# Attention and two projections merged into one hand-set TensorE order

## The chip, the core and the metric

The kernel runs on one core of one Trainium2 chip. The metric is the device time of one execution in microseconds (us); lower is better. The engines are named as the profile names them: PE is TensorE (PEld its weight loads), DVE is VectorE, ACT is ScalarE, POOL is GpSimd, SP is the engine that issues most of the DMAs.

## The reference

Inputs `q`, `k`, `v` are float32 of shape (8, 12, 448, 64): 8 batches, 12 heads, 448 positions, 64 channels. `w_in` is (768, 2048), `w_out` is (2048, 768).

```
q_n, k_n = rmsnorm(q, g_q), rmsnorm(k, g_k)       # x / sqrt(mean(x*x) + 1e-6) * g, over the 64 channels
scores   = q_n @ k_n.T / sqrt(64)                 # per batch and head: 448 x 448
attn     = softmax(scores);  o = attn @ v         # 448 x 64
x        = o of all heads side by side            # (3584 tokens, 768)
h        = x @ w_in                               # (3584, 2048)
g        = h * sigmoid(1.702 * h)
out      = g @ w_out                              # (3584, 768)
```

## The kernel before

The work falls into two stages, one after the other.

**Attention.** The unit is a pair of heads of one batch: 8 batches of 6 pairs make 48 pairs. The 448 positions are cut into 4 chunks of 112 rows. For each pair `phase1` issues four loads of q and k on SP (line 137), squares them on POOL (L143), sums the squares on DVE (L147) and loads v, cast to bf16, by two DMAs issued on POOL (L153). When all six pairs of a batch have their sums, `do_rsqrt` takes the reciprocal roots with integer and float steps on DVE (`_rsqrt_bits`, L26 to L38). `stage_T` scales q and k on POOL (L190), transposes them by 8 PE instructions (L199) and copies the result out of PSUM on DVE (L203). `stage_S` makes the scores in 4 chunks of keys: two matmuls with 64 contraction rows each, one for each head, in the two halves of the array (L214), then one exp on ACT for both heads (L221). `stage_Omm` multiplies the exps with v: 32 matmuls a pair, each with 112 columns of exps as weights and 65 moving columns (64 channels and a column of ones that gives the softmax sum, L231). `stage_Otail` divides on DVE (L244, L245), transposes back (4 PE instructions, L253) and copies into `xT` on ACT (L257). So a pair has 8 + 8 + 32 + 4 = 52 PE matmuls.

**Projections.** After all 48 pairs, in 7 blocks of 512 tokens: `gp` = 16 groups of 6 matmuls with `w_in_s` as weights and 512 moving columns (L311), sigmoid-gelu on ACT (L318), then `op` = 8 groups of 16 matmuls of 384 columns with the gelu output as weights (L328), a copy on ACT (L336), a store on SP (L337).

The order on each engine is set by a scheduler that takes the instructions by priority and by what they wait for; the program order of the loop over `gi` is the priority. Tiles come from pools with a number of buffers each; an instruction that writes a buffer waits until its last reader is done. PSUM has 8 banks; in the attention stage 4 of them are the two score buffers.

Of the kernel before, what the change touches and what calls it, by code (L numbers as in the profile page):

```python
# [13 lines left out]
AX = mybir.AxisListType  # L14

RSQRT_NEWTON = 2
_MAGIC = 0x5F3759DF


def _rsqrt_bits(nc, eng, out_ap, in_ap, magic_ap, tmp_pool, n_newton=2, tag=""):  # L20
    free_shape = list(in_ap.shape)
    sl = tuple(slice(0, d) for d in free_shape)
    x_int = in_ap.bitcast(I32)
    y = tmp_pool.tile(free_shape, FP32, tag="rsq_y" + tag, name="rsq_y")
    y_int = y[sl].bitcast(I32)
    eng.tensor_scalar(out=y_int, in0=x_int, scalar1=1, scalar2=None,  # L26
                      op0=ALU.arith_shift_right)
    eng.tensor_tensor(out=y_int, in0=magic_ap, in1=y_int, op=ALU.subtract)
    yf = y[sl]
    t = tmp_pool.tile(free_shape, FP32, tag="rsq_t" + tag, name="rsq_t")  # L30
    tf = t[sl]
    for i in range(n_newton):
        dst = out_ap if i == n_newton - 1 else yf
        eng.tensor_tensor(out=tf, in0=yf, in1=yf, op=ALU.mult)
        eng.tensor_tensor(out=tf, in0=tf, in1=in_ap, op=ALU.mult)
        eng.tensor_scalar(out=tf, in0=tf, scalar1=-0.5, scalar2=1.5,
                          op0=ALU.mult, op1=ALU.add)
        eng.tensor_tensor(out=dst, in0=yf, in1=tf, op=ALU.mult)  # L38
    if n_newton == 0:
        eng.tensor_copy(out=out_ap, in_=yf)  # L40
# [3 lines left out]
def kernel(  # L44
# [12 lines left out]

# [4 lines left out]
    NT = B * S  # L62
    SS = 112
    NS = S // SS
    NP = H // 2

    consts = ctx.enter_context(tc.tile_pool(name="consts", bufs=1))
    xt_pool = ctx.enter_context(tc.tile_pool(name="xt", bufs=1))
    wpool = ctx.enter_context(tc.tile_pool(name="w", bufs=1))

    ident = consts.tile([128, 128], BF16)
    make_identity(nc, ident)

    magicA = consts.tile([128, NP, 2, 2, NS], I32)
    nc.vector.memset(magicA[:, :, :, :, :], _MAGIC)

    gq128 = consts.tile([128, 1], FP32)
    gk128 = consts.tile([128, 1], FP32)
    gq_r = g_q.rearrange("(d o) -> d o", o=1)
    gk_r = g_k.rearrange("(d o) -> d o", o=1)  # L80
    nc.sync.dma_start(out=gq128[0:64, :], in_=gq_r)
    nc.sync.dma_start(out=gq128[64:128, :], in_=gq_r)
    nc.sync.dma_start(out=gk128[0:64, :], in_=gk_r)
    nc.sync.dma_start(out=gk128[64:128, :], in_=gk_r)
    gG = consts.tile([128, 1], FP32)
    nc.vector.tensor_tensor(out=gG[:, :], in0=gq128[:, :], in1=gk128[:, :],
                            op=ALU.mult)
    nc.vector.tensor_scalar(out=gG[:, :], in0=gG[:, :], scalar1=8.0,
                            scalar2=None, op0=ALU.mult)
    magicG = consts.tile([128, 1], I32)  # L90
    nc.vector.memset(magicG[:, :], _MAGIC)
    rs_pool = ctx.enter_context(tc.tile_pool(name="rs_const", bufs=1))
    gG_rs = consts.tile([128, 1], FP32)
    _rsqrt_bits(nc, nc.vector, gG_rs[:, :], gG[:, :], magicG[:, :], rs_pool,
                n_newton=3, tag="G")
    sqrtG128 = consts.tile([128, 1], FP32)
    nc.vector.reciprocal(out=sqrtG128[:, :], in_=gG_rs[:, :])

    w_in_s = wpool.tile([128, DM // 128, DF], BF16)
    nc.gpsimd.dma_start(  # L100
        out=w_in_s[:, :, :],
        in_=moe_w_in.rearrange("(ko p) f -> p ko f", p=128),
    )
    w_out_s = wpool.tile([128, DF // 128, DM], BF16)
    nc.gpsimd.dma_start(
        out=w_out_s[:, :, :],
        in_=moe_w_out.rearrange("(ko p) f -> p ko f", p=128),
    )

    xT = xt_pool.tile([128, DM // 128, NT], BF16)  # L110

    attn_pools = ExitStack()
    araw = attn_pools.enter_context(tc.tile_pool(name="a_raw", bufs=NP + 3))
    vraw = attn_pools.enter_context(tc.tile_pool(name="a_v", bufs=NP + 4))
    asqp = attn_pools.enter_context(tc.tile_pool(name="a_sq", bufs=2))
    astat = attn_pools.enter_context(tc.tile_pool(name="a_stat", bufs=2))
    asn = attn_pools.enter_context(tc.tile_pool(name="a_sn", bufs=3))
    asb2 = attn_pools.enter_context(tc.tile_pool(name="a_sb2", bufs=3))
    aobs = attn_pools.enter_context(tc.tile_pool(name="a_obs", bufs=2))

    ps_t = attn_pools.enter_context(
        tc.tile_pool(name="a_ps_t", bufs=1, space=bass.MemoryType.PSUM))
    ps_s = attn_pools.enter_context(
        tc.tile_pool(name="a_ps_s", bufs=2, space=bass.MemoryType.PSUM))
    ps_o = attn_pools.enter_context(
        tc.tile_pool(name="a_ps_o", bufs=2, space=bass.MemoryType.PSUM))
    ps_ot = attn_pools.enter_context(
        tc.tile_pool(name="a_ps_ot", bufs=1, space=bass.MemoryType.PSUM))

    def phase1(b, p, ssq):  # L130
        h0 = 2 * p
        qk_raw2 = araw.tile([128, 2, 2, NS, D], FP32, tag="qk_raw2",
                            name="qk_raw2")
        src = (q, k)
        for g in range(2):
            for hp in range(2):
                nc.sync.dma_start(  # L137
                    out=qk_raw2[:SS, g, hp, :, :],
                    in_=src[g][b, h0 + hp].rearrange(
                        "(ss ns) d -> ss ns d", ns=NS),  # L140
                )
        sqv = asqp.tile([128, 2, 2, NS, D], FP32, tag="sq", name="sq")
        nc.gpsimd.tensor_tensor(out=sqv[:SS, :, :, :, :],  # L143
                                in0=qk_raw2[:SS, :, :, :, :],
                                in1=qk_raw2[:SS, :, :, :, :],
                                op=ALU.mult)
        nc.vector.reduce_sum(out=ssq[:SS, p, :, :, :],  # L147
                             in_=sqv[:SS, :, :, :, :], axis=AX.X)
        v_ext2 = vraw.tile([128, 2, NS, D + 1], BF16, tag="v_ext2",
                           name="v_ext2")  # L150
        nc.gpsimd.memset(v_ext2[:SS, :, :, D:D + 1], 1.0)  # L151
        for hp in range(2):
            nc.gpsimd.dma_start(  # L153
                out=v_ext2[:SS, hp, :, :D],
                in_=v[b, h0 + hp].rearrange("(ss ns) d -> ss ns d", ns=NS),
            )
        return qk_raw2, v_ext2

    class BState:
        __slots__ = ("ssq", "aa", "qk", "vx")  # L160

        def __init__(self):
            self.ssq = astat.tile([128, NP, 2, 2, NS], FP32, tag="ssq",
                                  name="ssq")
            self.aa = None
            self.qk = [None] * NP
            self.vx = [None] * NP

    def do_rsqrt(st):
        st.aa = astat.tile([128, NP, 2, 2, NS], FP32, tag="aa", name="aa")  # L170
        _rsqrt_bits(nc, nc.vector, st.aa[:SS, :, :, :, :],
                    st.ssq[:SS, :, :, :, :], magicA[:SS, :, :, :, :], astat,
                    n_newton=RSQRT_NEWTON)

    states = [None] * (B + 1)
    states[0] = BState()
    for p in range(NP):
        qk, vx = phase1(0, p, states[0].ssq)
        states[0].qk[p] = qk
        states[0].vx[p] = vx  # L180
    do_rsqrt(states[0])

    def stage_T(b, i, st):
        qk_n2 = asn.tile([128, 2, NS, 2, D], BF16, tag="qkn", name="qkn")
        for g in range(2):
            in0 = st.qk[i][:SS, g, :, :, :].rearrange(
                "ss hp ns d -> ss ns hp d")
            in1 = st.aa[:SS, i, g, :, :].rearrange(
                "ss hp ns -> ss ns hp").to_broadcast([SS, NS, 2, D])
            nc.gpsimd.tensor_tensor(  # L190
                out=qk_n2[:SS, g, :, :, :],
                in0=in0,
                in1=in1,
                op=ALU.mult,
            )
        t_ps = ps_t.tile([128, 2, NS, SS], BF16, tag="tp", name="t_ps")
        for g in range(2):
            for s in range(NS):
                nc.tensor.transpose(t_ps[:128, g, s, :SS],  # L199
                                    qk_n2[:SS, g, s, :, :],  # L200
                                    ident[:SS, :SS])
        qkT = asb2.tile([128, 2, NS, SS], BF16, tag="qkT", name="qkT")
# [37 lines left out]
    def stage_Otail(b, i, oph):  # L240
# [11 lines left out]
        for qs in range(NS):  # L252
            nc.tensor.transpose(ot_ps[:128, qs, :SS], obs2[:SS, qs, :, :],  # L253
                                ident[:SS, :SS])
# [116 lines left out]
```

## Time and profile before

| | |
|---|---|
| median of 3 runs | 697.98 us (696.99 to 698.12) |
| span of the profiled execution, first to last instruction | 696.5 us |
| profiled execution's own time | its span and about 1.5 us around it, if it was like the median |
| PE busy | 618.6 us (89%), 4064 matmuls |
| DVE, ACT, POOL busy | 178.1, 313.5, 263.5 us |
| first matmul, first projection matmul, last matmul ends | 62.5, 398.9, 692.0 us |

A busy share is the time in which an engine had an instruction in work. For PE it says little of the speed: the instructions are pipelined, their ends are modelled, and a matmul at a slower array clock is busy for longer. So the prediction counts the distance between starts.

### The profile page before, as it was taken

Reading aid. Unit: us, or ns where it says so; the run is one execution under the profiler, and the core shown is the slowest. Engines: PE = TensorE matmul, PEld = TensorE weight load, DVE = VectorE, ACT = ScalarE, POOL = GpSimd, SP = SyncE. Lnnn points to the kernel's source line nnn. Section 1 sums busy time; section 2 is a strip of 40 time slices with the busy share of each in tenths; the row PEclk is TensorE's granted clock in tenths of the full one; section 3 lists DMA queues with packets and bytes.
Section 4 is the critical chain, followed back from the end, with each engine's and each line's share of the span. In section 5 each row is a group of like instructions: output and inputs, shape, how many; then the busy total and the mean of one; then the engine's idle time right before and its main releaser. Section 6 shows DMA issues by size and latency. Waiting matters only on the chain.

```text
span 696.5 us, 9788 instructions
## 1 busy us (share of the span) xinstructions
PE 618.6 (89%) x4064; PEld 386.2 (55%) x4064; DVE 178.1 (26%) x387; ACT 313.5 (45%) x382; POOL 263.5 (38%) x296
## 2 busy tenths in 40 slices
PE   0002799999999999999999999999999999999997
PEld 0001477677776767677777745555464554545554
DVE  1146463745347373633422200000000000000000
ACT  0001567666666666767676652332413233141331
POOL 1478959789595978959530000000000000000000
PEclk9999999999999999999999999999999999999999
DMA  8995627365362736434200001102011010101101
GB/s 152 234 244 79 123 20 147 45 122 73 53 137 18 143 50 116 78 31 84 14 1 1 1 1 47 46 0 91 1 46 45 24 69 0 69 24 46 46 23 70
DMA packets 76365, 45.48 MB, mean 65 GB/s; under 512 B 48416, under 2 KB 71968, under 8 KB 76320
## 3 DMA queue, kind: packets, MB, share of 16 engines
q0 software_dynamic: 47392, 11.80, 17.4%
q1 hardware_dynamic: 28928, 33.05, 15.3%
q8 instruction: 32, 0.52, 0.3%
q14 instruction: 13, 0.11, 0.0%
HBM read 45.61 MB, written 11.01 MB: 81 GB/s over the span
## 4 chain that ended last, share of the span: by engine, by line
PE 60%; POOL 19%; issue 8%; DMA 7%; DVE 5%; SPq 1%; ACT 0%; POOLq 0%; ACTq 0%
PE gp L311 21%; PE op L328 21%; PE o_ps L231 9%; POOL qkn L190 8%; POOL sq L143 7%; DMA qk_raw<-in_k_dram 6%; PE sc_ps L214 6%; POOL v_ext L153 4%; PE t_ps L199 2%; DVE rsq_y L26 2%; DVE ssq L147 1%; PE ot_ps L253 1%; DMA qk_raw<-in_q_dram 1%; POOL v_ext L151 0%; SPq L137 0%
## 5 line engine op out<-in xcount | busy, mean ns | idle before, releaser
L221 ACT ACTIVATE att<-sc_ps 112x896 bf16<-112x896 f32 x192 | 175.6, 921 | 175.6 <-PE sc_ps L214 174.2
L231 PEld LDWEIGHTS <-att 112*112 112x112 bf16 x1536 | 159.3, 210 | 36.3 <-issue 32.8
L231 PE MATMUL o_ps<-v_ext,att 112*112 112x65 bf16 x1536 | 175.7, 283 | 0.4 <-ACT att L221 0.3
L311 PE MATMUL gp<-xT,w_in_s 128*128 128x512 bf16 x672 | 148.3, 382 | 0.0
L328 PE MATMUL op<-w_out_s,g_tile 128*128 128x384 bf16 x896 | 146.7, 326 | 0.0
L328 PEld LDWEIGHTS <-g_tile 128*128 128x128 bf16 x896 | 87.7, 98 | 58.7
L214 PE MATMUL sc_ps<-qkT 64*112 64x448 bf16 x384 | 118.4, 617 | 0.8 <-DVE qkT L203 0.8
L199 PE MATMUL t_ps<-ident,qkn 112*128 112x112 bf16 x384 | 54.8, 295 | 68.6 <-POOL qkn L190 63.7
L311 PEld LDWEIGHTS <-w_in_s 128*128 128x128 bf16 x672 | 66.2, 99 | 79.2 <-issue 1.9
L190 POOL TENSOR_TENSOR qkn<-qk_raw,aa 112x512 bf16<-112x512 f32 x96 | 99.2, 1055 | 25.3 <-PE t_ps L199 13.3
L143 POOL TENSOR_TENSOR sq<-qk_raw 112x1024 f32<-112x1024 f32 x48 | 90.8, 1897 | 29.1 <-DMA qk_raw<-in_k_dram 27.4
L318 ACT ACTIVATE g_tile<-gp 128x512 bf16<-128x512 f32 x112 | 66.8, 597 | 74.7 <-PE gp L311 74.6
L199 PEld LDWEIGHTS <-qkn 112*128 112x128 bf16 x384 | 33.9, 136 | 97.5 <-POOL qkn L190 68.3
L336 ACT COPY osb<-op 128x768 f32<-128x768 f32 x28 | 22.4, 799 | 125.0 <-PE op L328 125.0
L147 DVE TENSOR_REDUCE ssq<-sq 112x16 f32<-112x1024 f32 x48 | 58.4, 1216 | 73.8 <-POOL sq L143 73.8
L153 POOL DMA_DIRECT2D v_ext<-in_v_dram x96 | 69.0, 723 | 11.0 <-POOL v_ext L151 10.1
L257 ACT COPY xT<-ot_ps 128x448 bf16<-128x448 bf16 x48 | 55.2, 1150 | 3.4 <-PE ot_ps L253 3.4
L203 DVE TENSOR_SCALAR qkT<-t_ps,sqrtG 128x896 bf16<-128x896 bf16 x48 | 32.6, 680 | 40.9 <-PE t_ps L199 40.9
L214 PEld LDWEIGHTS <-qkT 64*112 64x112 bf16 x384 | 31.8, 165 | 18.9 <-issue 8.3
L244 DVE RECIPROCAL rcp<-o_ps 112x4 f32<-112x4 f32 x96 | 17.0, 179 | 92.9 <-PE o_ps L231 92.9
L245 DVE TENSOR_TENSOR obs<-o_ps,rcp 112x256 bf16<-112x256 f32 x96 | 39.8, 420 | 1.5
L253 PE MATMUL ot_ps<-ident,obs 112*128 112x112 bf16 x192 | 27.6, 294 | 3.7 <-DVE obs L245 3.7
(28 smaller groups left out, 74.6 us busy)
## 6 DMA issues: line engine op xcount, KB each, us to landing
qk_raw<-in_q_dram SPq DMA_DIRECT2D x96, 112.0 KB, 2.3
qk_raw<-in_k_dram SPq DMA_DIRECT2D x96, 112.0 KB, 2.7
out_dram<-osb SPq DMA_DIRECT2D x28, 384.0 KB, 2.3
v_ext<-in_v_dram POOLq DMA_DIRECT2D x96, 56.0 KB, 2.9
w_in_s<-in_moe_w_in_dram POOLq DMA_DIRECT2D x1, 3072.0 KB, 21.3
w_out_s<-in_moe_w_out_dram POOLq DMA_DIRECT2D x1, 3072.0 KB, 40.8
gq<-in_g_q_dram SPq DMA_DIRECT2D x2, 0.2 KB, 2.3
gk<-in_g_k_dram SPq DMA_DIRECT2D x2, 0.2 KB, 8.0
```

The source lines that it names most:

```text
L143: nc.gpsimd.tensor_tensor(out=sqv[:SS, :, :, :, :], in0=qk_raw2[:SS, :, :, :, :], in1=qk_raw2[:SS, :, :, :, :], op=ALU.mult)
L147: nc.vector.reduce_sum(out=ssq[:SS, p, :, :, :], in_=sqv[:SS, :, :, :, :], axis=AX.X)
L153: nc.gpsimd.dma_start(out=v_ext2[:SS, hp, :, :D], in_=v[b, h0 + hp].rearrange("(ss ns) d -> ss ns d", ns=NS),)
L190: nc.gpsimd.tensor_tensor(out=qk_n2[:SS, g, :, :, :], in0=in0, in1=in1, op=ALU.mult,)
L199: nc.tensor.transpose(t_ps[:128, g, s, :SS], qk_n2[:SS, g, s, :, :], ident[:SS, :SS])
L214: nc.tensor.matmul(sc_ps[:SS, hp, :S], lhsT=qkT[lo:lo + 64, 1, kc, :SS], rhs=qkT[lo:lo + 64, 0, :, :], start=True, stop=True,)
L221: nc.scalar.activation(out=att2[:SS, kc, :, :], in_=sc_ps[:SS, :, :S], func=ACT.Exp)
L231: nc.tensor.matmul(oph[hp][:SS, qs, :D + 1], lhsT=att2[:SS, kc, hp, qs * SS:(qs + 1) * SS], rhs=st.vx[i][:SS, hp, kc, :D + 1], start=(kc = ...
L257: nc.scalar.copy(out=dst, in_=ot_ps[:, :, :])
L311: nc.tensor.matmul(gp[:, :], lhsT=w_in_s[:, ki, m * 128:(m + 1) * 128], rhs=xT[:, ki, tok0:tok0 + NTC], start=(ki == 0), stop=(ki == KI - 1),)
L318: nc.scalar.activation(out=g_tile[:, m, :], in_=gp[:, :], func=ACT.Gelu_apprx_sigmoid,)
L328: nc.tensor.matmul(op[:, half, :HALF], lhsT=g_tile[:, ko, tm * 128:(tm + 1) * 128], rhs=w_out_s[:, ko, half * HALF:(half + 1) * HALF], sta ...
```

## The change

It rewrites the kernel as one loop over the 48 pairs in which the PE order is exactly the program order (`manual_schedule` for PE; the other engines are still ordered by the scheduler).

- `fill(per_gap)` puts projection matmuls of batches whose attention is complete (`ready`) into four gaps of each pair. An item counts 190 or 165 ns in its own book-keeping and a gap takes items until 1525 ns are used up: 9 items of the first projection or 10 of the second. A batch becomes ready after the transposes back of its last pair, so the first batch is ready at the end of iteration 6, and batch 7 is left for after the loop.
- Projections go by batch: 448 moving columns in place of 512 in the first one; the second takes 3 blocks of 128 tokens after an even batch and 4 after an odd one.
- Gelu: h * sigmoid(1.702 h) = 0.5 h (1 + tanh(0.851 h)). ACT does the tanh, DVE the addition and product from PSUM (`scalar_tensor_tensor`), the factor 0.5 is in the copy of the output on ACT.
- Scores: the keys lie in `kz_ring`, with zeros in the 64 rows of the other head, so a score matmul has 128 contraction rows, and the two heads follow each other.
- Attention weights are loaded 128 columns at a time (`WIN`); the 16 extra result rows are not read.
- Loads: q and k of two heads in one DMA each, v in one more, all on SP; v is cast by DVE. Norms in groups of one pair for pairs 0, 1, 2, then of three pairs (`groups`). `w_in` and `w_out` are loaded by 6 and 4 DMAs on POOL after the first norm in program order.
- Before iteration i, `pre(i)` issues load(i + 6), stats(i + 5) and norm(i + 2). A group's root takes 11 DVE instructions on at most 48 values a row, where before a batch took 10 on 96.
- The copy into `xT` moves from ACT to DVE; the copy after the transpose becomes three DVE instructions (q, and k of each head).
- PSUM: 4 banks of scores, 1 for the attention output (`ps_o`), 3 for all else (`ps_w`: transposes both ways and both projections).

```diff
+    ctx.enter_context(tc.manual_schedule(engines={ENG.PE}))
...
+    groups = [[0], [1], [2], [3, 4, 5]] + [list(range(j, j + 3)) for j in range(6, NG, 3)]
...
+    def stats(i):
...
+        nc.gpsimd.tensor_tensor(out=sq[:SS], in0=raw[i][:SS], in1=raw[i][:SS], op=ALU.mult)
+        nc.vector.reduce_sum(out=ssq[:SS, i - grp[0]], in_=sq[:SS], axis=AX.X)
+        if i != grp[-1]:
+            return
...
+    def norm(i):
...
+        for gi in range(2):
+            nc.gpsimd.tensor_tensor(out=t[:SS, gi], in0=raw[i][:SS, gi].rearrange("p h n d -> p n h d"),
...
+                op=ALU.mult)
+        nc.vector.tensor_copy(out=vx_ring[i % N_V][:SS, :, :, :D], in_=vraw[i][:SS])
+    def T(i):
+        ps = ps_w.tile([128, 2, NS, SS], BF16, tag="w", name="t_ps")
...
+        nc.vector.tensor_copy(out=t[:, :], in_=ps[:, 0].rearrange("p n s -> p (n s)"))
+        for hp in range(2):
+            r = slice(64 * hp, 64 * hp + 64)
+            nc.vector.tensor_scalar(out=kz[r, hp, :], in0=kps[r], scalar1=gG[r, :],
+                                    scalar2=None, op0=ALU.mult)
+    def Sc(i, kc):
+        for hp in range(2):
+            nc.tensor.matmul(sc[:SS, hp, :S],
+                             lhsT=kz_ring[i % N_KZ][:, hp, kc * SS:(kc + 1) * SS],
+                             rhs=qT[i][:, :], start=True, stop=True)
+        nc.scalar.activation(out=att_ring[i % N_ATT][:SS, kc, :, :S],
+                             in_=sc[:SS, :, :S], func=ACT.Exp)
+    def PV(i, hp):
+        o = ps_o.tile([128, NS, D + 1], FP32, tag="o", name="o")
+        for qs in range(NS):
+            for kc in range(NS):
+                nc.tensor.matmul(o[:, qs, :],
+                                 lhsT=att[:SS, kc, hp, qs * SS:qs * SS + WIN],
+                                 rhs=vx[:SS, hp, kc, :],
+                                 start=(kc == 0), stop=(kc == NS - 1))
...
+    def OT(i):
...
+                        nc.scalar.activation(out=th[:, :], in_=ps[:, :], func=ACT.Tanh, scale=0.851)
+                        nc.vector.scalar_tensor_tensor(
+                            out=g_of[b // 2][:, m, lo:lo + S], in0=th[:, :], scalar=1.0,
+                            in1=ps[:, :], op0=ALU.add, op1=ALU.mult)
...
+                    def s2(ko, b=b, tm=tm, half=half, box=box, obox=obox):
...
+                        if ko == MI - 1:
+                            nc.scalar.mul(osb[:, half * HALF:(half + 1) * HALF], ps[:, :], 0.5)
...
+    LOAD, STAT, NORM = 6, 5, 2
+    per_gap = 36.6e3 / (NP * 4)
...
+    for i in range(NG + 1):
+        pre(i)
+        if i == 0:
+            T(0)
+        for s in range(NS):
+            if i < NG:
+                Sc(i, s)
+            if s == 0 and i > 0:
+                PV(i - 1, 0)
+            if s == 2 and i > 0:
+                PV(i - 1, 1)
+            fill(per_gap)
+            if s == 1 and i + 1 < NG:
+                T(i + 1)
+        if i > 0:
+            OT(i - 1)
+            if i % NP == 0:
+                ready = i // NP - 1
+    fill(1e12)
```

More of the change, by code (lines that the diff above doesn't have):

```diff
@@ L14 @@
 AX = mybir.AxisListType
-RSQRT_NEWTON = 2
+PSUM = bass.MemoryType.PSUM
+ENG = mybir.EngineType
 _MAGIC = 0x5F3759DF
[L20 to L40, printed above, removed]
 @with_exitstack
@@ L130, in phase1 @@
[L130 to L151, printed above, removed]
-        for hp in range(2):
[L153 to L157, printed above, removed]
@@ L175 @@
[L175 to L202, printed above, removed]
-        nc.vector.tensor_scalar(out=qkT[:, :, :, :], in0=t_ps[:, :, :, :],
-                                scalar1=sqrtG128[:, :], scalar2=None,
-                                op0=ALU.mult)
-        return qkT
@@ new lines @@
+    for t in vx_ring:
+        nc.gpsimd.memset(t[:, :, :, D:D + 1], 1.0)
+    for t in att_ring:
+        nc.gpsimd.memset(t[:, :, :, S:AW], 0.0)
+    wpool = pool("w", 1)
+    w_in_s = wpool.tile([128, KI, DF], BF16)
+    w_out_s = wpool.tile([128, MI, DM], BF16)
+    raw_p = pool("raw", 7)
+    vraw_p = pool("vraw", 7)
+    sq_p = pool("sq", 2)
+    stat_p = pool("stat", 3)
+    small_p = pool("small", 2)
+    qkn_p = pool("qkn", 3)
+    qT_p = pool("qT", 3)
+    obs_p = pool("obs", 2)
+    xt_p = pool("xt", 3)
@@ new lines @@
+    g_p = pool("g", 1)
+    th_p = pool("th", 3)
+    osb_p = pool("osb", 3)
+    ps_sc = pool("ps_sc", 2, space=PSUM)
+    ps_o = pool("ps_o", 1, space=PSUM)
+    ps_w = pool("ps_w", 3, space=PSUM)
+    raw = [None] * NG
+    vraw = [None] * NG
+    rs = [None] * NG
+    qkn = [None] * NG
+    qT = [None] * NG
+    obs = [None] * NG
+    xT = [None] * B
+    groups = [[0], [1], [2], [3, 4, 5]] + [list(range(j, j + 3)) for j in range(6, NG, 3)]
+    group_of = {p: g for g in groups for p in g}
@@ L336 @@
[L336 to L340 removed]
+                            start=(ko == 0), stop=(ko == MI - 1))
+                        if ko == MI - 1:
+                            osb = obox["o"]
+                            nc.scalar.mul(osb[:, half * HALF:(half + 1) * HALF], ps[:, :], 0.5)
+                            if half == 1:
+                                store(b // 2, tm, osb)
@@ new lines, in moe_list, with store @@
+                    for ko in range(MI):
+                        items.append((165, b, lambda f=s2, ko=ko: f(ko)))
+        return items
+    def store(bp, tm, osb):
+        c = tm * 128
+        while c < (tm + 1) * 128:
+            b, j = 2 * bp + c // S, c % S
+            ns, ss = j // SS, j % SS
+            n = min(SS - ss, (tm + 1) * 128 - c)
+            r = c - tm * 128
+            nc.sync.dma_start(
+                out=out[b * S:(b + 1) * S].rearrange("(ss ns) d -> ns ss d", ns=NS)[ns, ss:ss + n],
+                in_=osb[r:r + n, :])
+            c += n
```

346 lines of the change are left out of this document (163 added, 183 removed).

## The prediction, made before the changed kernel ran

> **What bounds the kernel now.** First the slices of the span on the page, to find the stages; then the stages by window; then the costliest groups.
>
> ```profile
> PE   0002799999999999999999999999999999999997
> DVE  1146463745347373633422200000000000000000
> POOL 1478959789595978959530000000000000000000
> PEclk9999999999999999999999999999999999999999
> ```
>
> Three stages: about 62 us without a matmul, attention up to 399 us (POOL and DVE in work too), projections with PE alone. The windows (PE, PEld, DVE, ACT, POOL busy with counts, then granted clock) say that PE is in work all the time in both later stages:
>
> ```profile
> 100.00:200.00 100.00, 98.33 (x760) 70.35 (x760) 47.81 (x110) 68.67 (x74) 80.99 (x91) 1.00 0.52 91
> 200.00:300.00 100.00, 98.10 (x756) 69.92 (x756) 55.17 (x113) 65.92 (x73) 80.44 (x87) 1.00 0.50 83
> ```
>
> 1516 matmuls in 200 us at 52 a pair are 29.2 pairs: 6.86 us a pair. But "in work" is not "fast". The first projection matmuls, looked up by line in two windows (min/median/max ns):
>
> ```profile
> L311 PE MATMUL gp<-xT,w_in_s x9: 618/634/634, 398.9 to 402.7; 128*128 128x512 bf16 x9
> L311 PE MATMUL gp<-xT,w_in_s x87: 379/379/410, 403.1 to 421.7; 128*128 128x512 bf16 x87
> ```
>
> The same matmul takes 634 ns for the first 4 us after attention and 379 ns from then on, though the granted clock reads full in every slice. So attention left the array at a slow clock, and 4.2 us of dense work ended it. The chain (start, us, what) gives the distances:
>
> ```profile
> 399.09 2.13 PE gp L311 x5
> ...
> 422.07 20.80 PE op L328 x128
> 442.87 20.72 PE gp L311 x96
> ...
> 671.19 20.82 PE op L328 x128
> ```
>
> Slow, 512 columns take 2.13/5 = 0.426 us. Fast, 20.72/96 = 0.216 for 512 columns and 20.80/128 = 0.1625 for 384: 0.42 ns a column, so 0.189 for 448. [...] The attention stage in detail (start, length):
>
> ```profile
> 202.24 0.62 PE L214 MATMUL sc_ps<-qkT 64*112 64x448 bf16 x2
> 202.79 1.33 PE L231 MATMUL o_ps<-v_ext,att 112*112 112x65 bf16 x12
> 204.05 0.62 PE L214 MATMUL sc_ps<-qkT 64*112 64x448 bf16 x2
> 204.60 0.74 PE L199 MATMUL t_ps<-ident,qkn 112*128 112x112 bf16 x6
> 205.99 1.66 PE L231 MATMUL o_ps<-v_ext,att 112*112 112x65 bf16 x16
> ```
>
> ```profile
> L231 PE MATMUL o_ps<-v_ext,att 112*112 112x65 bf16 x1536 | 175.7, 283 | 0.4 <-ACT att L221 0.3
> L199 PE MATMUL t_ps<-ident,qkn 112*128 112x112 bf16 x384 | 54.8, 295 | 68.6 <-POOL qkn L190 63.7
> ```
>
> Of 16 value matmuls in 1.66 us the last is recorded with 0.283, so starts are (1.66 - 0.283)/15 = 0.092 us apart. From one score pair to the next, 204.05 - 202.24 = 1.81 us, there are 12 of them, so a score pair takes 0.70. Six transposes: (0.74 - 0.295)/5 = 0.09. Per pair 32 x 0.092 + 4 x 0.70 + 12 x 0.09 = 6.8, the 6.86 above. PE's steps bound this stage.
>
> **Part by part.** *PE, attention, at the fast clock.* Scores: 8 matmuls of 448 columns with the full contraction, 8 x 0.189 = 1.51 us instead of 2.8. Value matmuls: the trace has no such step, so bounds: 0.092 (nothing gained by 128 columns) and 65 x 0.42 = 0.027. The records of weight loads:
>
> ```profile
> L231 PEld LDWEIGHTS <-att 112*112 112x112 bf16 x1536 | 159.3, 210 | 36.3 <-issue 32.8
> L328 PEld LDWEIGHTS <-g_tile 128*128 128x128 bf16 x896 | 87.7, 98 | 58.7
> ```
>
> A load of 128 columns is recorded with 98 ns (at the fast clock), one of 112 with 210 (at the slow one). The step is now set by the load, so I scale it, 0.092 x 98/210 = 0.043, and take 0.045 (an estimate): 1.44 us a pair. [...] Transposes lie between 0.047 (112 columns fast) and 0.093; 0.07 x 12 = 0.84. Together 3.8 us a pair (2.9 to 5.6).
>
> *PE, projections.* A batch has 96 x 0.189 + 112 x 0.1625 (96 and 128 in turn) = 36.3 us, 6.06 a pair: unchanged in total (291 us), only moved under the attention work. PE needs 9.85 us a pair.
>
> *DVE.* It now has much more to do. Rows:
>
> ```profile
> L147 DVE TENSOR_REDUCE ssq<-sq 112x16 f32<-112x1024 f32 x48 | 58.4, 1216 | 73.8 <-POOL sq L143 73.8
> L203 DVE TENSOR_SCALAR qkT<-t_ps,sqrtG 128x896 bf16<-128x896 bf16 x48 | 32.6, 680 | 40.9 <-PE t_ps L199 40.9
> L244 DVE RECIPROCAL rcp<-o_ps 112x4 f32<-112x4 f32 x96 | 17.0, 179 | 92.9 <-PE o_ps L231 92.9
> L245 DVE TENSOR_TENSOR obs<-o_ps,rcp 112x256 bf16<-112x256 f32 x96 | 39.8, 420 | 1.5
> ```
>
> Sum of squares 1.22; four PSUM copies of 448 (half of 680 plus a start-up, 0.44 each) 1.76; reciprocals 0.36; products 0.84; cast of v 0.45; root, 11 steps of about 0.2 for three pairs, 0.73: 5.36 us. The gelu product from PSUM: on the line from 256 columns (420) to 1024 (1216), 448 cost 0.62; 2.67 a pair are 1.65. So 7.0, plus waits for POOL. Those are seen in the root (min/median/max ns), and in one case in time:
>
> ```profile
> L26 DVE TENSOR_SCALAR rsq_y<-ssq x8: 179/3326/4001, 50.0 to 332.9; 112x96 int32<-112x96 int32 x8
> ...
> 208.74 4.00 DVE L26 TENSOR_SCALAR rsq_y<-ssq 112x96 int32<-112x96 int32 x1
> 208.85 3.75 POOL L143 TENSOR_TENSOR sq<-qk_raw 112x1024 f32<-112x1024 f32 x2
> ```
>
> A step of 0.18 us lasts 4.0 while POOL squares. Root groups come twice as often, and the cast of v is such a step too: I put 1.0 a pair for each, between 0 and POOL's 4.0 (1.9 + 2 x 1.06 below). DVE then has 9.0 us a pair, close to PE's 9.85.
>
> ```profile
> L190 POOL TENSOR_TENSOR qkn<-qk_raw,aa 112x512 bf16<-112x512 f32 x96 | 99.2, 1055 | 25.3 <-PE t_ps L199 13.3
> L143 POOL TENSOR_TENSOR sq<-qk_raw 112x1024 f32<-112x1024 f32 x48 | 90.8, 1897 | 29.1 <-DMA qk_raw<-in_k_dram 27.4
> L221 ACT ACTIVATE att<-sc_ps 112x896 bf16<-112x896 f32 x192 | 175.6, 921 | 175.6 <-PE sc_ps L214 174.2
> L318 ACT ACTIVATE g_tile<-gp 128x512 bf16<-128x512 f32 x112 | 66.8, 597 | 74.7 <-PE gp L311 74.6
> L336 ACT COPY osb<-op 128x768 f32<-128x768 f32 x28 | 22.4, 799 | 125.0 <-PE op L328 125.0
> ...
> v_ext<-in_v_dram POOLq DMA_DIRECT2D x96, 56.0 KB, 2.9
> ```
>
> *ACT*: 4 x 0.92, 2.67 tanh of 0.54 (597 less 64 columns, at (921 - 597)/384 ns each), 1.17 half copies of about 0.48 (799 less 384 columns at the same slope): 5.7 us a pair, not a bound. *POOL* loses 96 DMA issues and keeps 4.0. *SP* gets the v loads and has them in one queue with the stores, which wait for ACT's copy; loads stand behind them. But they are issued six pairs ahead, some 60 us, and land in 3: hidden. Without that lead each pair would wait about 3 us for its loads.
>
> *A gap of the merged stage.* With 9 first-projection items PE needs 3.8/4 + 9 x 0.189 = 2.65 us, DVE 7.36/4 + 1.5 x 0.62 = 2.77; with 10 second-projection items PE 2.58, DVE 1.84. A batch fills 10.7 and 11.2 gaps and leaves 2.1 empty (DVE 1.84): 29.6 + 28.9 + 3.9 = 62.4, 10.4 us a pair. A POOL wait of 3 to 4 us outlasts the three `ps_w` banks (a group of six takes 1.13 us), so PE stalls behind the unread bank: 0.6 a pair. I take 11.0.
>
> *Start.*
>
> ```profile
> 5.19 17.30 DMA qk_raw<-in_k_dram
> ...
> 62.53 0.56 PE L199 MATMUL t_ps<-ident,qkn 112*128 112x112 bf16 x4 [62.53 <-POOL qkn L190]
> ```
>
> The root no longer waits for six pairs. The first pair lands between 6 us and the 22.5 seen here beside the weight loads; with square, sum, root and norm (1.9 + 1.2 + 2.4 + 2.1) the first transpose comes at about 20 us: 14 if the weight loads really follow the first norm on POOL, 31 if the scheduler, finding POOL idle, issues them at once as now. Seven pairs then run without fill: PE is slow there (8 x 0.373 + 32 x 0.06 + 12 x 0.09 = 6.0 us), DVE needs 5.36 + 2.0 = 7.4, so 52 us, and the first batch is ready at 72 us.
>
> *End.* After pair 47: its rest 2.3, batch 7 with 96 x 0.189 + 128 x 0.1625 = 38.9, and 4.5 us after the last matmul as now (692.0 to 696.5): 46.
>
> *Sum.* 20 + 52 + 41 x 11.0 + 46 = 569 us of span against 696.5; the median stands 1.5 above the profiled span, so 570.
>
> **Rivals.** *PE alone bounds*: the waits for POOL fall between PE's needs. For it: DVE's sum is below PE's. Against: PE's order is fixed, and DVE serves it first come. With a start of 65 (pairs of 6.4, half the waits): 65 + 41 x 9.85 + 46 = 515.
>
> *The array falls back to the slow clock.* For it: attention, PE 98% in work, never left that state; its streams (32 x 65 + 4 x 448 + 12 x 112 columns at twice 0.42 ns) filled 4.4 of 6.86 us, 63%; projections fill 100%; the merged stage about 9.0 of 11.0, 82%, between the two. Against: slow, PE would be filled wholly and so leave it again within 4 us. Slow half of the time, PE does three quarters: 9.85/0.75 = 13.1 a pair, 72 + 538 + 46 = 656. [...]
>
> *Slower: table loads on ACT.*
>
> ```profile
> L221 ACT ACT_TABLE_LOAD x1 | 1.3, 1283 | 0.7 <-PEq L355 0.7
> L318 ACT ACT_TABLE_LOAD x1 | 1.3, 1283 | 0.0
> ```
>
> Exp and the gelu needed one load each; if exp and tanh do too, they alternate in 75 first-projection gaps. Three loads a gap make ACT 0.92 + 0.81 + 3.85 = 5.6 us against 2.77: 570 + 75 x 2.8 = 780. It decides from 2.1 loads a gap on. Against: ACT's copies needed none. [...]
>
> **How the numbers follow.** Forecast 58% (535 to 605), PE alone 17%, slow clock 18%, table loads 4%, other 3%. The range 512 to 640 leaves out the loads, the worse third of the slow cases and a few of the fast. A measurement of this kernel tells about 0.2% from no change; all cases but the loads and one in a hundred are faster: 0.95, 0.01, 0.04.
>
> **What would show it.** In the changed profile: no table loads beyond one or two; projection matmuls of 448 columns at about 0.189 us distance, medians well below 634 ns; value matmuls near 0.045; first matmul near 20 us, first projection matmul near 72; DVE above 80% of the merged stage, and PE idle there behind DVE by about 1 us a pair. The prediction fails if the array is slow in the merged stage, if DVE's long steps follow POOL more often than put here, or if the start takes 100 us.

## The result, and the profile after

The changed kernel takes 606.52 us (median of 4 runs, 605.55 to 607.28) against 698.05 us for the kernel before: a ratio of 0.869, with an interval of 0.868 to 0.870. The forecast was 570, with 512 to 640 as its range. Span of the profiled execution: 604.0 us.

The slices of the page of the changed kernel:

```profile
PE   0144657898588897978698888789869999999996
...
PEclk9996688999799998889988899798979999999999
```

PE starts 45 us earlier than before (first matmul at 17.8 us instead of 62.5) and attention and projections now run together, but it isn't the row of nines that the kernel before had: it stands at 4 to 7 in the first slices and dips every few slices up to the thirtieth. The granted clock dips in or beside the same slices. The windows by stage (busy us with counts for PE, PEld, DVE, ACT, POOL, then granted clock, DMA share, GB/s), and below them the windows of the score line L197 alone (PE, PEld, clock, DMA share, GB/s), of which a pair has 8:

```profile
20.00:92.00 72.00, 34.93 (x341) 23.46 (x342) 55.18 (x131) 25.36 (x29) 49.69 (x38) 0.83 0.85 189
92.00:440.00 348.00, 294.12 (x2542) 180.64 (x2539) 204.42 (x494) 162.88 (x230) 119.14 (x91) 0.94 0.28 79
440.00:548.00 108.00, 102.61 (x932) 65.69 (x930) 57.16 (x142) 61.26 (x88) 20.33 (x18) 0.97 0.12 35
```

```profile
92.00:440.00 348.00, 66.33 (x232) 26.69 (x232) 0.94 0.28 79
440.00:548.00 108.00, 24.08 (x88) 9.91 (x88) 0.97 0.12 35
```

232/8 = 29 pairs in 348 us are 12.0 us a pair while loads still run; 88/8 = 11 pairs in 108 us are 9.8 once they are over. No engine is near full in the first of these: PE 85%, DVE 59%, ACT 47%, POOL 34%. Where everything is idle part of the time, the time is in waits. The waits (engine and line, what it waited for: us in total, times, longest), then SP's own queue:

```profile
POOL sq L139 <- DMA raw<-in_k_dram: 159.6, 32, 10.3
POOL qkn L169 <- PE t_ps L182: 115.3, 25, 7.9
DVE ssq L140 <- POOL sq L139: 94.2, 29, 5.9
PE ot_ps L225 <- DVE obs L216: 41.2, 20, 5.5
```

```profile
SPq L123 <- POOL qkn L169: 218.0, 33, 13.6
...
SPq L127 <- DVE obs L216: 58.7, 21, 10.5
```

PE waits for DVE's copies (`obs`), DVE waits for POOL's squares, POOL waits for loads, and the loads wait in SP's queue until their buffers are free: POOL's norm frees that of q and k (L123), DVE's cast that of v (L127; the profile names `obs`, which comes right behind the cast). That is a ring, and the chain (start, us, what) goes round it once every pair:

```profile
281.92 0.43 DVE vx L175
...
283.26 4.39 DMA raw<-in_k_dram
...
287.77 1.90 POOL sq L139
...
289.70 1.22 DVE ssq L140
...
292.29 0.43 DVE vx L175
...
293.13 3.68 DMA raw<-in_k_dram
...
296.97 1.90 POOL sq L139
...
298.90 1.22 DVE ssq L140
```

One turn takes about 10 us, and a load of some 4 us stands in it, although the program issues each load six pairs ahead. The scheduler had moved the square forward in POOL's queue: counted in the trace, the square of pair 33 stands directly ahead of the norm of pair 27, where the program has the square of pair 30. There are seven buffers, so that norm frees the one that pair 34's load needs, and it stands behind a wait for the load of pair 33. In the turn shown the chain goes through the cast: the norm ends at 291.70 and lets the load of q go, but in SP's queue the load of k stands behind a load of v, which goes when the cast ends at 292.72. Both stand behind the same square. The timeline shows what hangs on it: the first row is the sum's wait, the second PE's wait behind it.

```profile
298.90 1.22 DVE L140 TENSOR_REDUCE ssq<-sq 112x16 f32<-112x1024 f32 x1 [3.85 <-POOL sq L139]
302.30 0.56 PE L225 MATMUL ot_ps<-ident,obs 112*128 112x112 bf16 x4 [5.38 <-DVE obs L216]
303.40 1.09 PE L210 MATMUL o<-vx,att 112*128 112x65 bf16 x16
304.30 2.93 PE L243 MATMUL gp<-xt,w_in_s 128*128 128x448 bf16 x9
307.44 1.86 PE L243 MATMUL gp<-xt,w_in_s 128*128 128x448 bf16 x9
309.92 0.68 PE L210 MATMUL o<-vx,att 112*128 112x65 bf16 x16
```

The last four rows are the array's clock, recorded at 0.5 from 299.6 to 306.5 us. The same 9 matmuls take 2.93 us right after a 5.4 us wait and 1.86 three microseconds later; the same 16 value matmuls 1.09 and 0.68, so their starts are (1.09 - 0.262)/15 = 0.055 and (0.68 - 0.194)/15 = 0.033 us apart (0.262 and 0.194 are the longest and shortest of them). Of the 768 first-projection matmuls 85 have the slow distance (0.373 us), of the 384 score matmuls 51 (33 of them before 92 us): 136 x 0.184 = 25 us.

### The profile page after: what moved, and what is told of

It reads as the page before. It is cut to its first block, busy times and chain, and to the rows that moved or that the text cites. A ratio compares the mean times of both kernels' runs of the same rounds, so it can differ in the third digit from the quotient of the medians.

```text
span 604.0 us, 10291 instructions
## 1 busy us (share of the span) xinstructions
PE 482.9 (80%) x4160; PEld 299.7 (50%) x4160; DVE 336.6 (56%) x815; ACT 268.4 (44%) x377; POOL 197.3 (33%) x167
## 4 chain that ended last, share of the span: by engine, by line
PE 37%; DVE 22%; DMA 20%; POOL 13%; SPq 5%; issue 2%; POOLq 0%; ACT 0%
DMA raw<-in_k_dram 18%; PE gp L243 18%; PE op L269 9%; POOL sq L139 8%; DVE ssq L140 6%; POOL qkn L169 5%; PE sc L197 5%; SPq L123 4%; PE o L210 3%; DVE kz L190 2%; DVE g L252 2%; DVE obs L216 2%; DMA vraw<-in_v_dram 2%; DVE vx L175 2%; PE t_ps L182 1%
## 5 line engine op out<-in xcount | busy, mean ns | idle before, releaser
L200 ACT ACTIVATE att<-sc 112x896 bf16<-112x896 f32 x192 | 175.2, 917 | 224.6 <-PE sc L197 223.9
L243 PE MATMUL gp<-xt,w_in_s 128*128 128x448 bf16 x768 | 175.1, 377 | 26.8 <-DVE g L252 26.8
L269 PE MATMUL op<-w_out_s,g 128*128 128x384 bf16 x896 | 159.8, 326 | 0.0
L139 POOL TENSOR_TENSOR sq<-raw 112x1024 f32<-112x1024 f32 x48 | 90.8, 1894 | 178.3 <-DMA raw<-in_k_dram 159.6
L169 POOL TENSOR_TENSOR qkn<-raw,rs 112x512 bf16<-112x512 f32 x96 | 99.8, 1061 | 139.6 <-PE t_ps L182 115.3
L197 PE MATMUL sc<-qT,kz 128*112 128x448 bf16 x384 | 114.9, 384 | 7.9 <-DVE kz L190 7.6
L269 PEld LDWEIGHTS <-g 128*128 128x128 bf16 x896 | 85.0, 98 | 54.5
L252 DVE SCALAR_TENSOR_TENSOR g<-th,gp 128x448 bf16<-128x448 f32 x128 | 78.5, 615 | 51.9 <-ACT th L249 51.9
L249 ACT ACTIVATE th<-gp 128x448 f32<-128x448 f32 x128 | 69.4, 542 | 75.5 <-PE gp L243 75.4
L210 PE MATMUL o<-vx,att 112*128 112x65 bf16 x1536 | 68.6, 199 | 9.2 <-DVE obs L216 9.2
L197 PEld LDWEIGHTS <-kz 128*112 128x112 bf16 x384 | 45.0, 142 | 20.6 <-DVE kz L190 8.9
L225 PE MATMUL ot_ps<-ident,obs 112*128 112x112 bf16 x192 | 18.9, 225 | 41.4 <-DVE obs L216 41.2
```

Of the source, the lines that this page charges most:

```text
L139: nc.gpsimd.tensor_tensor(out=sq[:SS], in0=raw[i][:SS], in1=raw[i][:SS], op=ALU.mult)
L169: nc.gpsimd.tensor_tensor(out=t[:SS, gi], in0=raw[i][:SS, gi].rearrange("p h n d -> p n h d"), in1=y[:SS, a, gi].rearrange("p h n -> p n h ...
L197: nc.tensor.matmul(sc[:SS, hp, :S], lhsT=kz_ring[i % N_KZ][:, hp, kc * SS:(kc + 1) * SS], rhs=qT[i][:, :], start=True, stop=True)
L200: nc.scalar.activation(out=att_ring[i % N_ATT][:SS, kc, :, :S], in_=sc[:SS, :, :S], func=ACT.Exp)
L210: nc.tensor.matmul(o[:, qs, :], lhsT=att[:SS, kc, hp, qs * SS:qs * SS + WIN], rhs=vx[:SS, hp, kc, :], start=(kc == 0), stop=(kc == NS - 1))
L243: nc.tensor.matmul(ps[:, :], lhsT=w_in_s[:, ki, m * 128:(m + 1) * 128], rhs=xT[b][:, ki, :], start=(ki == 0), stop=(ki == KI - 1))
```

## The experiments

Edits are to the changed kernel where nothing else is said. Ratios are to the kernel before.

**POOL in program order.** The theory is the ring above: the scheduler's order on POOL makes it. The rival has the drops of PE's clock as the cause.

```diff
-    ctx.enter_context(tc.manual_schedule(engines={ENG.PE}))
+    ctx.enter_context(tc.manual_schedule(engines={ENG.PE, ENG.Pool}))
```

> Edit: POOL too keeps its program order (square of pair i+5, then norm of pair i+2), nothing else. Theory A (a ring through the queues): in the changed kernel POOL was given the square of a pair just loaded ahead of the norm that frees the next load's buffer, so norm, load, square, sum follow each other once a pair and DVE waits with PE's copies behind the sum (DVE waited 94 us for squares, SP 218 us for norms). Program order puts the square one iteration after its load: those two waits fall under 30 us each, pairs 7 to 35 go from about 12 to about 10 us, and the time to 535 to 560 us. [...] Theory C (PE's clock drops cause the loss): 606 within 2%, the same number of slow projection matmuls (85 of 768).

556.00 us, 0.797 (0.796 to 0.798): 50 us less from one word, where the rival had 606. Its waits, and its score line's window:

```profile
POOL sq L139 <- DMA raw<-in_k_dram: 5.8, 1, 5.8
DVE ssq L140 <- POOL sq L139: 55.8, 39, 3.4
SPq L123 <- POOL qkn L169: 182.4, 31, 10.1
```

```profile
92.00:498.00 406.00, 86.97 (x320) 35.24 (x320) 1.00 0.27 76
```

POOL's wait for loads is gone (159.6 to 5.8 us), and 40 pairs take 10.15 us each instead of 11.4. Two of the expected numbers missed: SP still waits 182 us for norms, harmless now because the loads come early enough all the same, and DVE still waits 55.8 us for squares, since each square now runs directly ahead of its sum. DVE's order, still the scheduler's, changed along with POOL's (between 100 and 430 us the sum stood ahead of the query copy in 10 of 28 pairs, now in none), so the 50 us are the worth of the whole edit and not of POOL's queue alone. The slow first-projection matmuls fall from 85 to 8, and the slow score matmuls behind 92 us from 18 to none, with nothing done to PE's order, while its waits fell (the transposes back for `obs` from 41.2 to 23.3 us, the first projection for `g` from 26.8 to 1.9): the lapses of the clock went with PE's waits here. Ahead of 92 us, where nothing fills PE, 44 of 58 score matmuls are slow still (33 in the changed kernel).

**One more buffer for the loads.** If the ring is a matter of order, a longer lead only moves it; if buffers are short, it pays.

```diff
-    raw_p = pool("raw", 7)
-    vraw_p = pool("vraw", 7)
+    raw_p = pool("raw", 8)
+    vraw_p = pool("vraw", 8)
```

> Edit: 8 buffers in place of 7 for the loaded q, k and v. Theory A (ring): the order on POOL is still norm of an old pair, load into its buffer, square of the new pair, next norm, so one pair more of lead changes nothing: 606 within 1%, SP still waits over 150 us for norms. Rival D (just too few buffers): a seventh more lead gives a pair's time back more often; SP's wait for norms falls by a third or more and the time to 575 to 595.

595.29 us (591.08 to 598.17), 0.853: 1.9% better, between the two.

```profile
SPq L123 <- POOL qkn L169: 203.6, 31, 13.5
POOL sq L139 <- DMA raw<-in_k_dram: 135.4, 31, 6.5
```

SP's wait falls by 7%, not by the third that shortage asked for, and POOL still waits 135 us for loads. The time lies at the upper end of what shortage asked for, so neither theory has both numbers right. The trace says why the ring stays: with eight buffers the scheduler moved the square one pair further forward (pair 35's stands ahead of pair 28's norm), and that norm again frees the buffer for the next load. The buffer gives slack to the ring; the order makes it.

**112 columns of weights in place of 128.**

```diff
-    WIN = 128
+    WIN = SS
...
-                nc.tensor.matmul(o[:, qs, :],
+                nc.tensor.matmul(o[:SS, qs, :],
```

> Edit: the value matmuls load 112 columns of weights again (result rows 112), the rest as in the changed kernel. The step measured 0.033 us with 128 columns. Theory E (128 columns made the step short): it becomes 0.06 to 0.093, PE needs 0.9 to 1.9 us a pair more, and since PE waits about 2 us a pair in the merged stage, part is hidden: 615 to 660. Theory F (the faster array clock made it short, 0.092 was the slow clock): the step is 0.047 or less and the time 606 within 2%.

612.74 us (605.11 to 614.45), 0.875: about 1% slower than the changed kernel, hardly beyond its own scatter. Two groups of 16 value matmuls in its timeline:

```profile
441.73 0.97 PE L210 MATMUL o<-vx,att 112*112 112x65 bf16 x16
449.12 1.66 PE L210 MATMUL o<-vx,att 112*112 112x65 bf16 x16
```

1.66 us is to the digit the group of the kernel before, 0.092 a step; at the fast clock a step is 0.052. So neither theory held alone: taken in this order, of the fall from 0.092 to 0.033 the clock made 0.040 and the 128 columns 0.019, or 0.6 us a pair of 32. That the time hardly moved may be because part of it hides in PE's waits.

**Gelu from ACT's own table.** It puts the table loads of the third rival on the chip: the gelu of the kernel before, which had a load of its own there beside exp's (1.28 us each), directly from PSUM, without DVE's product.

```diff
-                        nc.scalar.activation(out=th[:, :], in_=ps[:, :], func=ACT.Tanh, scale=0.851)
-                        nc.vector.scalar_tensor_tensor(
-                            out=g_of[b // 2][:, m, lo:lo + S], in0=th[:, :], scalar=1.0,
-                            in1=ps[:, :], op0=ALU.add, op1=ALU.mult)
+                        nc.scalar.activation(out=g_of[b // 2][:, m, lo:lo + S], in_=ps[:, :],
+                                             func=ACT.Gelu_apprx_sigmoid)
```

> Edit: the sigmoid-gelu of the kernel before on ACT straight from PSUM, in place of tanh on ACT and addition and product on DVE; factor 0.5 is 1.0. Exp and this gelu each had a table load of 1.28 us before. Theory (the rival of the prediction): they alternate in about 75 gaps with first-projection groups, 2 to 3 loads a gap, 150 to 250 loads, ACT needs 4.3 to 5.6 us a gap against 2.9: 680 to 780 us. Rival: the scheduler gathers exps and gelus, under 100 loads, and DVE, freed of 79 us, makes up for it: 590 to 640.

691.44 us, 0.990 (0.987 to 0.993): nearly the whole gain is gone. Groups of this kernel:

```profile
L199 ACT ACT_TABLE_LOAD x78 | 100.1, 1283 | 10.3 <-PE sc L196 8.3 <-PEq L366 0.7
L248 ACT ACT_TABLE_LOAD x78 | 100.1, 1283 | 1.4
```

156 loads are 200 us of ACT, although DVE is spared 78 us. In the changed kernel there is one load in all:

```profile
L200 ACT ACT_TABLE_LOAD x1 | 1.3, 1283 | 0.7 <-PEq L371 0.7
```

That one load serves 192 exps and 128 tanhs.

**The 128 columns in the kernel before.** Would they alone bring the clock back there?

```diff
+    att_ring = [consts.tile([128, NS, 2, 464], BF16, ...) for j in range(3)]   # 16 columns of zeros
...
-                        oph[hp][:SS, qs, :D + 1],
-                        lhsT=att2[:SS, kc, hp, qs * SS:(qs + 1) * SS],
+                        oph[hp][:, qs, :D + 1],
+                        lhsT=att2[:SS, kc, hp, qs * SS:qs * SS + 128],
```

> Edit: the kernel before, with 128 columns of attention weights (zeros behind the last query chunk), nothing else of the change. Theory E (the load sets the step in the slow-clock attention stage): the step falls from 0.092 to about 0.055 (65 columns at the slow clock), 48 x 32 x 0.037 = 57 us, so 640; where POOL, busy 5.6 of 6.86 us a pair there, takes over, 650 to 660. Theory F (clock alone): no change, 698. In both the attention matmuls stay at the slow clock, as nothing fills PE.

659.83 us, 0.946 (0.940 to 0.952). Its timeline has both clocks, and its window shows how full the engines are:

```profile
217.11 1.03 PE L236 MATMUL o_ps<-v_ext,att 112*128 112x65 bf16 x15
227.57 0.48 PE L236 MATMUL o_ps<-v_ext,att 112*128 112x65 bf16 x10
```

```profile
100.00:359.00 259.00, 210.38 (x2257) 135.95 (x2255) 137.33 (x309) 187.54 (x216) 199.36 (x220) 0.65 0.46 75
```

The step is 0.054 at the slow clock and 0.033 at the fast one. 254 of the 384 score matmuls are still slow, where before all were: theory E had the time right, but not that all would stay slow. PE is in work 81% of the time, POOL 77% and ACT 72%, so no engine is full. The 128 columns, with the part of the fast clock that came with them, are worth 38 us; the other 53 us of the changed kernel's gain come from the rest of the change.

**Scores without padding**, with POOL in program order: 64 contraction rows for each head again.

```diff
-                             lhsT=kz_ring[i % N_KZ][:, hp, kc * SS:(kc + 1) * SS],
-                             rhs=qT[i][:, :], start=True, stop=True)
+                             lhsT=kz_ring[i % N_KZ][64 * hp:64 * hp + 64, hp, kc * SS:(kc + 1) * SS],
+                             rhs=qT[i][64 * hp:64 * hp + 64, :], start=True, stop=True)
```

> On the kernel with POOL in program order (556 us), scores again with 64 contraction rows for each head in its half of the array; keys are still written to the padded buffers. [...] Rival: at the fast clock two heads side by side cost 0.19 plus little, up to 0.15 less than padded: 530 to 550.

559.88 us (559.19 to 564.24), 0.804 against 0.797: 0.8% slower. In its timeline:

```profile
253.35 0.40 PE L197 MATMUL sc<-qT,kz 64*112 64x448 bf16 x2
```

The two heads start 3 ns apart, but the next matmul comes only 0.33 us later (at 253.68), and one ahead of such a pair waits 0.14 us in place of 0.05: about 0.42 us a pair of scores against 2 x 0.189 = 0.378 with padding. So the padded pair, with twice the rows, is 0.04 us shorter, and the rival's 530 to 550 us was not met. What makes these gaps no run singles out. Of the 0.70 us that the prediction read in the kernel before, 0.28 were the clock.

**No filling**, with POOL in program order: all projections after the pairs, with the buffers that this needs (8 of `xt`, 5 of each load).

```diff
-            fill(per_gap)
```

> On the kernel with POOL in program order (556 us), no projections in the gaps: all of them after the last pair (output tiles of all 8 batches kept; 5 load buffers, 1 square and 2 output buffers to make room). Theory H (merging is worth the time in which attention would leave PE short): attention alone runs at DVE's 5.4 to 6.5 us a pair, and its matmuls mostly at the slow clock; first batch ready near 92, then 41 x 6.0 = 246, then 291 + 5: 634 (610 to 660). Rival (merging is worth nothing, the shorter steps are everything): 41 x 4 = 164, so 552 to 570.

652.26 us, 0.934 (0.929 to 0.939). The window of its attention:

```profile
96.00:344.00 248.00, 167.55 (x2087) 118.34 (x2086) 193.61 (x527) 143.20 (x160) 149.42 (x113) 0.84 0.33 96
```

2087 matmuls at 52 a pair are 40.1 pairs in 248 us, 6.2 us each, with PE 68% in work, DVE 78%. The projections follow alone. This is what theory H had. Merging is worth 652 - 556 = 96 us, with the price of the fewer load buffers in it: it puts projection matmuls into time in which attention leaves PE idle.

**The start: weights loaded later**, with POOL in program order. Are the first pairs slow because the weight loads take the DMA engines?

```diff
+        if i in (1, 2, 3):
+            for ki in (2 * i - 2, 2 * i - 1):
+                nc.gpsimd.dma_start(out=w_in_s[:, ki, :], in_=moe_w_in[ki * 128:(ki + 1) * 128, :])
+        if i in (4, 5, 6, 7):
...
```

> On the kernel with POOL in program order (556 us), the DMAs of the projection weights are moved from before the first iteration to iterations 1 to 3 (w_in) and 4 to 7 (w_out). Theory I (the start is a queue for DMA bandwidth: 230 to 240 GB/s up to 60 us, weights and the first pairs' loads share it): pairs 1 to 6 land earlier, the first batch is ready at 65 to 75 us in place of 92: 532 to 542. Rival (DVE and POOL chains set the start, not DMA): 92 stays, 556 within 1%; or w_out comes late for the first second-projection group and PE waits there.

552.60 us (552.35 to 552.62), 0.792. The first projection matmul by line, and the window of 40 to 60 us, here and then in the kernel with POOL in program order:

```profile
L243 PE MATMUL gp<-xt,w_in_s x768: 349/352/578, 89.0 to 524.5; 128*128 128x448 bf16 x192
```

```profile
40.00:60.00 20.00, 11.59 (x104) 7.77 (x104) 13.88 (x36) 7.11 (x8) 15.54 (x16) 1.00 0.76 165
```

```profile
40.00:60.00 20.00, 6.83 (x70) 4.20 (x67) 14.29 (x29) 5.50 (x6) 17.51 (x15) 1.00 1.13 229
```

229 GB/s became 165, the load of pair 8's k landed at 30.2 us instead of 47.6, and PE got more done in this window (104 matmuls against 70). But little of it lasted: the first projection came at 89.0 instead of 91.4, and the time is 3.4 us less. Bandwidth was worth some 2 us of the start and not the 17 to 27 that were expected; that theory fell.

**Even gaps**: after the pairs that a batch needs, two gaps stay empty. Eight items a gap spread them.

```diff
-    per_gap = 36.6e3 / (NP * 4)
+    per_gap = 1520
```

> On the kernel with POOL in program order and late weights (552.6 us): a gap takes items until 1520 in place of 1525 ns are used up, so 8 in place of 9 first-projection matmuls (10 of the second as before). Theory J (9 a gap use a batch's work up before the next batch is ready; pairs then last 12.7, 11.5, 9.8, 9.9, 9.6 and 8.8 or 5.4 us, and in the last one PE waits for DVE and the exps): the pairs even out near 9.6 to 10.0, and 41 pairs gain 0.3 to 0.6 us each: 530 to 542. Rival: PE has the same work either way and the waits only move: 552 within 1%.

562.03 us, 0.805: 9.4 us slower than the last kernel, where a gain was expected. One wait of its timeline, and that wait summed over the span, here and then in the last kernel:

```profile
298.79 1.22 DVE L140 TENSOR_REDUCE ssq<-sq 112x16 f32<-112x1024 f32 x1 [1.45 <-POOL sq L139]
299.93 1.14 DVE L252 SCALAR_TENSOR_TENSOR g<-th,gp 128x448 bf16<-128x448 f32 x2
300.60 0.36 PE L225 MATMUL ot_ps<-ident,obs 112*128 112x112 bf16 x4 [1.74 <-DVE g L252]
```

```profile
PE ot_ps L225 <- DVE g L252: 28.8, 17, 2.6
```

```profile
PE ot_ps L225 <- DVE g L252: 16.7, 11, 2.2
```

The transposes back need a bank that holds a projection's result; its reader on DVE stands behind a sum that waits for POOL's square. This wait grew by 12 us. The empty gaps seem to have been the slack in which DVE caught up.

**POOL's order at the start**, with even gaps: at the start each norm goes behind the next pair's square, later ahead of it; pair 3 is a group of its own.

```diff
-                if j <= NORM:
-                    norm(j)
+                if j <= NORM + 1:
+                    norm(j - 1)
```

> The same, and POOL's program order at the start is changed: the square of pair j+1 before the norm of pair j, pair 3 is a group of its own, and from iteration 1 the norm comes before the square. Theory K (the start is a chain: POOL waits 4 to 7 us in each of the first norms for DVE's sum and root, and the later squares stand behind it): the first batch is ready at 68 to 80 us in place of 89, 10 to 20 us less than the kernel with even gaps. Rival (DVE's own work, or the loads, set the start): 86 to 89, no more than 3 us less.

553.22 us (553.04 to 553.47), 0.793; a single further run gave 552.99.

```profile
L243 PE MATMUL gp<-xt,w_in_s x768: 349/352/577, 79.8 to 524.9; 128*128 128x448 bf16 x192
```

The first projection moves from 89.0 to 79.8 and the time falls by 8.8 us, a little less than the 10 to 20 expected: what the start saves, the end keeps. What the edit does behind the start changes nothing (318 score matmuls take 412 us, 413 before). So POOL's order is part of what makes the start slow.

**DVE in program order too.**

```diff
-    ctx.enter_context(tc.manual_schedule(engines={ENG.PE, ENG.Pool}))
+    ctx.enter_context(tc.manual_schedule(engines={ENG.PE, ENG.Pool, ENG.DVE}))
```

> The kernel with the changed start, with DVE too in program order. Theory A (in-order queues: what stands ahead of PE's PSUM copies decides): in program order the sum and the root of pair i+5 stand ahead of the copies of iteration i, PE waits for them at the start of each iteration, 1 to 3 us a pair: 20 to 80 us more. Rival: the scheduler's placing is no better than program order: within 2%.

533.34 us (530.93 to 534.19), 0.764 (0.762 to 0.766): the fastest of all, 20 us less than the kernel that it edits, and the opposite of the loss that was expected; the rival's 2% is passed too. Its score line's window, and its waits:

```profile
85.00:470.00 385.00, 87.18 (x318) 35.38 (x318) 0.99 0.28 79
```

```profile
DVE ssq L140 <- POOL sq L139: 1.8, 1, 1.8
PE sc L197 <- DVE kz L190: 23.9, 1, 23.9
```

39.75 pairs in 385 us are 9.7 a pair, near what PE itself needs. The sum, put where the program has it, no longer waits for the square (54.8 us in the kernel that it edits, 1.8 here), so no copy stands behind such a wait; what PE's transposes back wait for DVE falls from 42.4 to 4.8 us. The start got worse (first projection at 84.4 instead of 79.8): in program order DVE does all early sums first, and PE waits 23.9 us for its first keys. A start like that of the kernel before this one with this steady state was not tried.

## Why the prediction was right or wrong

**PE's steps** were right and a little pessimistic. Projections stand at 0.189 and 0.1625 as predicted, scores at 0.189, transposes at 0.05 (0.07 predicted), value matmuls at 0.033 (0.045 predicted): 1.51 + 32 x 0.033 + 12 x 0.052 + 6.06 = 9.3 us a pair, not 9.85. The scaled recorded load, 98/210, was a fair guide to the step.

**DVE** was over-sized. It was in work 336.6/48 = 7.0 us a pair, with the lengthened steps in it; the prediction had 7.0 without them and 2.0 more for them. That term measures 0.65. By shape, the cast and the first of the root's eleven lines:

```profile
L175 DVE CAST vx<-vraw 112x512 bf16<-112x512 f32 x48 | 25.5, 532 | 16.8 <-DMA vraw<-in_v_dram 15.6
L150 DVE TENSOR_SCALAR ssq<-ssq 112x48 f32<-112x48 f32 x15 | 9.7, 650 | 0.0
```

The eleven lines add to 57.5 us over 15 groups, 3.83 a group against 11 x 0.2; that is 0.54 a pair, and the cast's 0.10 more (0.53 against a median of 0.43). POOL was at work 80% of the attention stage before and is at 34% of the merged one, which may be why, with less of it for DVE to run into; no run singles this out.

**The merged pair** was put at 11.0 us and took 11.4 over 40 pairs. The number is near for the wrong reason. The prediction had DVE's work and its waits for POOL as the limit of a gap, and DVE above 80% as a sign of it; measured, DVE was in work 59% of the stage up to 440 us. The step that failed is the one on SP, by which the loads are issued six pairs ahead, land in 3 us and are hidden. The prediction's own condition (without that lead each pair would wait about 3 us) is what happened: the loads were late in time though early in the program, because SP's next load waited for buffers that POOL's norm and DVE's cast free, and both stood behind the square and the sum of the pair just loaded. The program-order runs show it: 10.15 us with POOL put right, 9.7 with DVE too. That 606.5 lies in the range is thus partly luck: PE and DVE were put too high, and the wait for loads, which the sum had at nothing, more than made up for it. It lies just outside the 535 to 605 that had the 58%.

**Start**: the first transpose came at 17.8 us (20 predicted), and the first weight load was issued right behind the first norm, at 18.8, so that doubt was settled on the good side. The failed step is the seven pairs of 7.4 us: the first projection came at 92.2 instead of 72. The first 9.2 us went to a cast of pair 3 that stood on DVE ahead of the copies of pair 0:

```profile
25.88 0.43 DVE L175 CAST vx<-vraw 112x512 bf16<-112x512 f32 x1 [9.23 <-DMA vraw<-in_v_dram]
```

From the first score at 27.0 on the seven pairs took 9.2 us each, not 7.4. That cast alone isn't the cause: with POOL in program order the first score comes at 20.2, but the first projection still at 91.4. Late weights gave 2 us and POOL's order at the start 9; what holds the rest, 79.8 against 72, stays open.

**End**: 46 predicted, 46.8 measured (from the end of pair 46's transposes back at 557.2 to 604.0). So the 35 us by which the sum was short are 20 of the start, 41 x 0.34 = 14 of the pairs and 1 of the end.

**The rivals.** *PE alone bounds* (9.85 a pair, 9.3 by the measured steps) comes near the kernel once loads are over (9.8) and the last kernel (9.7); the changed kernel's order keeps it from there. *The slow clock* came true in small: 136 slow matmuls of 1152, not half of the time. The changed kernel's slow matmuls come behind waits of up to 5.5 us, but in the kernel without filling 87 score matmuls behind 96 us are slow though no wait of PE there is over 2.9 us; what makes the clock fall no run singles out. *Table loads* did not occur. Put on the chip they cost 85 us: 156 loads are 2.1 a gap, for which the prediction's formula gives some 120 (210 is for three). DVE was spared 78 us, and part of the loads may lie in time in which ACT had been waiting; no run separates the two.

## What to carry to other kernels

When one engine's order is written by hand, look at the order the scheduler then gives the others: an instruction that frees a buffer must not stand, on any in-order queue, behind one that waits for the load into such a buffer. "Issued six pairs ahead" says nothing of when a load lands; the wait of the instruction that uses it does (here POOL's square, 159.6 us and then 5.8, while SP's own wait only fell from 218 to 182). The stage in which no engine was above 85% was bound by waits here, and the chain showed the ring that repeats; mending it also brought the array's clock back (0.94 to 1.00 in the windows from 92 us on).

## What the runs showed of the hardware

- The granted clock read 1.00 throughout the kernel before, while all its attention matmuls had the slow distance; in the changed kernel it falls (0.83 to 0.97) where slow matmuls are. The traces show why the row differs: the first record of the clock stands at 403.2 us in the kernel before, where its matmuls become fast, and at 43.6 in the changed one, and ahead of it the row reads 1.00 for want of a record. All slow matmuls counted above lie ahead of that record or run, two of them only in part, in stretches recorded at 0.5, of 3.4 or 6.8 us each. The distance between starts was the sure sign in both.
- 128 columns of weights give shorter steps than 112: 0.033 against 0.052 us at the fast clock, 0.054 against 0.092 at the slow one.
- Transposes of 112 columns ran at 0.049 us a step at the fast clock, against 0.09 in the kernel before: the clock sets their step too.
- Padding a contraction from 64 to 128 rows made a pair of scores shorter (0.378 against 0.42 us) beside matmuls that use the whole array.
